# Mixing products interleaved one by one with attention head pairs

## The chip, the cores and the metric

The kernel runs on one core of a Trainium2 chip. Of its engines five matter here: TensorE (PE in the profile, with PEld for its weight loads), VectorE (DVE), ScalarE (ACT), GpSimd (POOL), and the DMA queues, of which SyncE's (SP) carries the transposing transfers and the output. The engines run side by side, each through its own list of instructions in order, and wait for each other through semaphores. The metric is the device time of one execution in microseconds. Before the change it is 171.31 us, the median of three runs (171.11 to 171.92).

## The reference: what is computed

Two layers follow each other, on a batch of 4, with 8 heads, 768 positions and a head width of 64 (model width 512).

The first is an attention in which each position sees its last 96 positions and the first 8, with a bias that falls linearly with the distance:

```python
scores = scale * np.matmul(q, k.transpose(0, 1, 3, 2))
keep = is_global | is_local            # first 8 positions, or 0 <= i - j < 96
scores = np.where(keep, scores + bias, -1000000000.0)
a = np.exp(scores - np.max(scores, axis=-1, keepdims=True))
a = a / (np.sum(a, axis=-1, keepdims=True) + 1e-09)
x = np.matmul(a, v)                    # heads side by side: (4, 768, 512)
```

The second mixes positions and then channels:

```python
theta = x @ w_theta
zr, zi = x * np.cos(theta), x * np.sin(theta)
y = np.einsum('ts,bsd->btd', w_tok_r, zr) + np.einsum('ts,bsd->btd', w_tok_i, zi)
u = x + y
out = u + np.maximum(u @ w_ch, 0.0)
```

## The kernel before, in words

Positions are cut into six tiles of 128, channels into four blocks of 128. All matrix work is in bfloat16 and adds up in PSUM, the memory that only TensorE's matmuls write and that VectorE and ScalarE read.

**Attention of a head pair.** For two heads at a time, `att_transpose` turns q and k (64 wide, so two heads share the 128 rows); ScalarE copies the result out of PSUM (line 232, two copies) and GpSimd makes a variant of the keys with the 8 global positions in front (lines 257 and 258). Since each query tile sees only its own and the previous key tile, the scores are eleven 128 x 128 blocks per head, in three groups (`GROUPS`): group 0 for query tiles 0 and 1, group 1 for tiles 2 and 3, group 2 for tiles 4 and 5. `att_scores` (line 297) computes a group for both heads in one PSUM tile, ScalarE takes the exponential (line 306), and VectorE multiplies by a precomputed mask (lines 317 and 319). `att_values` multiplies the probabilities by the values (line 346, 22 matmuls of 65 columns; the 65th column gives the sum), and VectorE divides (lines 353 and 354).

**Mixing.** `mix_theta` and `mix_z` make the cosine and sine products. `mix_tok` builds an output tile of 128 positions out of twelve matmuls of 512 columns (six source tiles times real and imaginary part; line 430). I call such a matmul a product. When a tile has its twelve, VectorE adds x (line 435), which makes u, and the SP queue transposes u by DMA. `mix_ch` takes four more such products with `w_ch` (line 472), VectorE adds and clips (line 475), and SP writes the result out.

**The order of the work.** `K` keeps the program order on every engine, so the order of the calls in the source is the order of execution. The mixing of batch b is laid beside the attention of batch b + 1, for b = 0, 1, 2. I call these three pieces stretches 1, 2 and 3; each goes through four head pairs. `tok_units` lists the mixing as units, each of four products of a tile (or all four of a `mix_ch`), and `attend_beside` hands them out with `m(n)`:

- ahead of the first pair: three units (twelve products) in stretches 2 and 3, none in stretch 1;
- in each pair: first score group, then two units (one in the first pair), then score groups 1 and 2, the transposes of the next pair, two units (all but one of those left in the last pair), the values;
- behind the last pair: the last unit.

In stretches 2 and 3 the list begins with eight products of tile 0 and eight of tile 1, then the last four of tile 0, the last four of tile 1, then tiles 2 to 5 in turn, with `mix_ch(0)` behind tile 3 and `mix_ch(1)` behind tile 4. In stretch 1 tiles 0 and 1 have ten of their twelve products from earlier, so the list begins with two products of each.

**PSUM buffers.** Mixing tiles and `mix_ch` tiles take turns in two buffers (`ps_mm`, from `ps_acc`), so a tile's first product waits until VectorE has read the tile before the last. Scores, values and `mix_theta` share two wider ones (`ps_w`, from `ps_wide`). Behind each stretch come `mix_ch(2)`, the transposes of the last quarter of x (`turn_x`, line 378), `mix_ch(3)`, and then `mix_theta` for the next batch.

The functions that the change touches:

Of the kernel before, what the change touches and what calls it, by code (L numbers as in the profile page):

```python
# [16 lines left out]
def kernel(  # L17
# [14 lines left out]
    B, H, S, D = q.shape  # L32
    T = 128
    NT = S // T
# [24 lines left out]
    def ps_acc():  # L59
        return psum.tile([T, DM], FP, name="ps_mm", tag="ps_mm", bufs=2)  # L60
# [264 lines left out]
    def att_values(b, h0, apart=False):  # L325

        if h0 == 0:
            x_sb[b] = mbuf.tile([T, NC, NT, T], BF, name="x_sb", bufs=2)
            xTs[b] = mbuf.tile([T, NC, S], BF, name="xT", bufs=2)
        xp = x_sb[b][:, h0 // 2, :, :]  # L330
        vs, vp = v_sb[b % 2], v_pv[b % 2]
        po = None if apart else ps_wide()
        for hh in range(2):
            h = h0 + hh
            ph = ps_acc() if apart else po[:, hh, :]
            for it in range(NT):
                dst = ph[:, it * (D + 1):(it + 1) * (D + 1)]
                mms = []
                if it >= 1:
                    g_, i_ = where[(it, 1)]  # L340
                    rhs = vs[:, h, 0, :] if it == 1 else vp[:, h, it - 2, :]
                    mms.append((probs[b, h0, g_][:, hh, i_ * T:(i_ + 1) * T], rhs))
                g_, i_ = where[(it, 0)]
                mms.append((probs[b, h0, g_][:, hh, i_ * T:(i_ + 1) * T], vs[:, h, it, :]))
                for i_, (lhsT, rhs) in enumerate(mms):
                    K(nc.tensor.matmul(dst, lhsT=lhsT, rhs=rhs,  # L346
                                       start=(i_ == 0), stop=(i_ == len(mms) - 1)))
            if apart:
                values[b, h] = ph
        if not apart:  # L350
            pv = po[:, :, 0:NT * (D + 1)].rearrange("a h (t d) -> a h t d", d=D + 1)
            rec = abuf.tile([T, 2, NT, 1], FP, name="rec")
            K(nc.vector.reciprocal(rec, pv[:, :, :, D:D + 1]))
# [14 lines left out]
    def turn_x(b, dc, by_dma, eng=nc.vector.tensor_copy):  # L368

        xT = xTs[b][:, dc, :]  # L370
        if by_dma:
            K(nc.sync.dma_start(out=xT.rearrange("a (c t) -> a c t", t=T),
                                in_=x_sb[b][:, dc, :, :].rearrange("a t d -> a (t d)"),
                                transpose=True))
            return
        pt = ps_tr(S)
        for st in range(NT):
            K(nc.tensor.transpose(pt[:, st * T:(st + 1) * T], x_sb[b][:, dc, st, :], ident))  # L378
# [81 lines left out]
        for s2 in range(n):  # L460
            uTs[b, tt + s2] = (uT, n, s2)

    def mix_ch(b, tt, cuts=(DM,)):
        uT, n, s2 = uTs[b, tt]
        out_t = out[b].rearrange("(t p) d -> p t d", p=T)[:, tt, :]
        for c0, c1 in zip((0,) + cuts, cuts):
            N = c1 - c0
            cols = slice(c0, c1)
            pc = ps_acc()
            for dc in range(NC):  # L470
                c = (n * dc + s2) * T
                K(nc.tensor.matmul(pc[:, 0:N], lhsT=uT[:, c:c + T], rhs=w_ch_bf[:, dc, cols],  # L472
                                   start=(dc == 0), stop=(dc == NC - 1)))
            o_sb = mbuf.tile([T, N], FP, name="o_sb", bufs=4)
            K(nc.vector.scalar_tensor_tensor(o_sb, in0=pc[:, 0:N], scalar=0.0,  # L475
                                             in1=us[b][:, tt, cols], op0=ALU.max, op1=ALU.add))
            K(nc.sync.dma_start(out=out_t[:, cols], in_=o_sb))


    def tok_units(b, lead):  # L480


        L = []

        def piece(tt, s0):
            L.append(lambda: mix_tok(b, tt, PAIRS[s0:s0 + 4]))

        for tt in (0, 1):
            for s0 in (0, 4) if lead else ():
                piece(tt, s0)  # L490
        for tt in range(NT):
            if tt > 1:
                for s0 in (0, 4, 8):
                    piece(tt, s0)
            elif lead:
                piece(tt, 8)
            else:
                L.append(lambda tt=tt: mix_tok(b, tt, [(4, 1), (5, 1)]))
            if tt in (3, 4):
                L.append(lambda tt=tt: mix_ch(b, tt - 3))  # L500
        return L

    def attend_beside(b, main, lead, load):


        def m(n=1):
# [24 lines left out]


    for h in range(H):
# [71 lines left out]
    for b in range(B):  # L605
        if b == B - 1:
            main = tok_units(b, True)
            main.insert(-1, lambda: mix_uT(b, 4, 1, "act"))
# [58 lines left out]
```

## Time and profile before

| | |
|---|---|
| median of three runs | 171.31 us (171.11 to 171.92) |
| the profiled execution | 171.33 us, of which 169.5 us are the profile's span |
| TensorE matmuls busy | 158.7 us, 94% of the span |
| VectorE busy | 114.7 us, 68% |
| ScalarE busy | 103.0 us, 61% |
| GpSimd busy | 63.2 us, 37% |
| mean granted clock of TensorE | 1.00 |
| products of line 430, 288 in all | 67.0 us |

A line of the chain or of the timeline gives the start in microseconds from the start of the span, a duration, the engine, what it writes or reads with the line of the kernel, and how many instructions are put together. A matmul's duration there is longer than its share of the engine, because matmuls overlap; the distance between starts tells what one costs. Some matmul records are missing from a trace, so a row can say seven where the program has eight. Where the start of an engine's piece is given in square brackets with an arrow, the engine was idle for that time and the name tells what ended it.

The stretches run, from the first scores of their first pair to the end of the values of their last pair, from 39.47 to 62.05 us, from 75.20 to 98.38 us and from 111.53 to 134.38 us.

### The profile page before, as it was taken

What the parts mean: (1) busy time and instruction counts of PE and PEld (TensorE: products, weight loads), DVE (VectorE), ACT (ScalarE), POOL (GpSimd) and SP (SyncE); (2) the same over time, 40 slices, a digit from 0 to 9 for tenths busy, and PEclk for the clock granted to TensorE, in tenths of its full rate; (3) what the DMA queues carried; (4) which work ended last, traced back from release to release, by engine and by line L of the source; (5) the groups of instructions that cost most, each with busy time, mean ns of one, the idle gap of its engine ahead of it and who ended that gap; (6) DMA issues with size and microseconds to landing.
All of it is one profiled execution on the core that took longest, in us unless ns stands there. A gap on an engine that the chain in (4) does not pass through costs nothing.

```text
span 169.5 us, 4624 instructions
## 1 busy us (share of the span) xinstructions
PE 158.7 (94%) x1965; PEld 86.2 (51%) x1988; DVE 114.7 (68%) x210; ACT 103.0 (61%) x120; POOL 63.2 (37%) x99
## 2 busy tenths in 40 slices
PE   7779999999899999999999999999999999999992
PEld 2346665555465654446555554445655544444440
DVE  7768875965858875767587694849568756534362
ACT  4989887957686562798658615996765618300010
POOL 8996797004484650032972900054245000000000
PEclk9999999999999999999999999999999999999999
DMA  4999999999999999910599999711953342121325
GB/s 148 194 180 190 209 211 208 198 180 182 158 140 196 141 173 215 257 70 4 92 145 170 155 187 197 210 62 37 73 110 95 99 148 86 68 60 34 113 102 186
DMA packets 57060, 24.08 MB, mean 142 GB/s; under 512 B 43088, under 2 KB 54096, under 8 KB 57040
## 3 DMA queue, kind: packets, MB, share of 16 engines
q0 software_dynamic: 35328, 12.45, 65.5%
q1 hardware_dynamic: 21440, 10.95, 31.2%
q10 hardware_dynamic: 272, 0.39, 0.7%
q8 instruction: 15, 0.25, 0.6%
q14 instruction: 5, 0.04, 0.1%
HBM read 25.69 MB, written 6.29 MB: 189 GB/s over the span
## 4 chain that ended last, share of the span: by engine, by line
PE 80%; DVE 6%; DMA 4%; issue 3%; POOL 3%; ACT 3%; DVEq 0%; ACTq 0%; POOLq 0%
PE ps_mm L430 35%; PE ps_mm L472 12%; PE ps_w L395 11%; PE ps_w L297 7%; PE ps_w L346 5%; DMA v_sb<-in_v_dram 4%; PE ps_tr L226 3%; PE ps_mm L346 2%; ACT e L306 2%; PE ps_tr L114 2%; DVE zri L411 1%; DVE w_tokT L117 1%; PE ps_tr L378 1%; DVE p L319 1%; ACT qk L249 1%
## 5 line engine op out<-in xcount | busy, mean ns | idle before, releaser
L430 PE MATMUL ps_mm<-zri,w_tokT 128*128 128x512 bf16 x276 | 67.0, 380 | 1.3 <-issue 0.8
L306 ACT ACTIVATE e<-ps_w 128x1024 bf16<-128x1024 f32 (+1 forms) x40 | 37.1, 958 | 17.8 <-PE ps_w L297 17.8
L430 PEld LDWEIGHTS <-w_tokT 128*128 128x128 bf16 x288 | 26.2, 98 | 30.3 <-issue 2.3
L257 POOL COPY qk<-qk 128x512 bf16<-128x512 bf16 x15 | 9.5, 636 | 65.2 <-ACT qk L232 53.0
L319 DVE TENSOR_TENSOR p<-e,wmask 128x1024 bf16<-128x1024 bf16 x28 | 19.9, 712 | 11.8 <-ACT e L306 11.8
L403 ACT ACTIVATE cs<-ps_w,halfpi 128x1024 bf16<-128x1024 f32 x12 | 13.4, 1116 | 18.6 <-PE ps_w L395 18.6
L435 DVE TENSOR_TENSOR u<-x_sb,ps_mm 128x512 bf16<-128x512 bf16 x24 | 16.2, 683 | 12.2 <-PE ps_mm L430 12.2
L395 PE MATMUL ps_w<-w_theta_bf,xT 128*128 128x512 bf16 x91 | 22.6, 379 | 0.6 <-ACT cs L404 0.3
L411 DVE TENSOR_TENSOR zri<-cs,x_sb 128x1024 bf16<-128x1024 bf16 x24 | 16.1, 688 | 9.1 <-ACT cs L403 7.7
L472 PE MATMUL ps_mm<-w_ch_bf,uTd 128*128 128x512 bf16 x82 | 21.5, 379 | 0.6 <-issue 0.5
L297 PE MATMUL ps_w<-qk 64*128 64x128 bf16 (+1 forms) x320 | 16.1, 223 | 2.3 <-DVE qk L249 0.8
L475 DVE SCALAR_TENSOR_TENSOR o_sb<-ps_mm,u 128x512 f32<-128x512 f32 (+2 forms) x25 | 16.5, 664 | 1.1 <-PE ps_mm L472 0.9
L232 ACT COPY qk<-ps_tr 128x768 bf16<-128x768 bf16 x21 | 16.0, 815 | 2.0 <-issue 2.0
L297 PEld LDWEIGHTS <-qk 64*128 64x128 bf16 x320 | 10.0, 94 | 12.1 <-issue 7.8
L346 PEld LDWEIGHTS <-p 128*128 128x128 bf16 x352 | 13.2, 97 | 4.6 <-DVE p L319 0.8
L395 PEld LDWEIGHTS <-xT 128*128 128x128 bf16 x96 | 9.0, 98 | 10.8 <-issue 0.5
L80 POOL DMA_DIRECT2D v_sb<-in_v_dram x10 | 13.0, 1299 | 0.0
L472 PEld LDWEIGHTS <-uTd 128*128 128x128 bf16 x88 | 8.2, 98 | 9.0 <-issue 0.2
L404 ACT ACTIVATE cs<-ps_w 128x1024 bf16<-128x1024 f32 x12 | 12.2, 1020 | 0.0
L92 POOL COPY v_pv<-v_sb 8x520 bf16<-8x520 bf16 x15 | 11.5, 767 | 0.9
L354 DVE TENSOR_TENSOR x_sb<-ps_w,rec 128x768 bf16<-128x768 f32 x12 | 11.5, 958 | 0.4
L346 PE MATMUL ps_w<-v_sb,p 128*128 128x65 bf16 x168 | 11.3, 193 | 0.0
(84 smaller groups left out, 180.2 us busy)
## 6 DMA issues: line engine op xcount, KB each, us to landing
out_dram<-o_sb SPq DMA_DIRECT2D x23, 256.0 KB, 2.3
q_sb<-in_q_dram POOLq DMA_DIRECT2D x6, 384.0 KB, 6.2
k_sb<-in_k_dram POOLq DMA_DIRECT2D x6, 384.0 KB, 9.0
v_sb<-in_v_dram POOLq DMA_DIRECT2D x6, 384.0 KB, 13.5
w_nat<-in_moe_w_tok_r_dram POOLq DMA_DIRECT2D x1, 1152.0 KB, 12.3
w_nat<-in_moe_w_tok_i_dram POOLq DMA_DIRECT2D x1, 1152.0 KB, 13.4
v_sb<-in_v_dram POOLq DMA_DIRECT2D x4, 192.0 KB, 6.7
q_sb<-in_q_dram POOLq DMA_DIRECT2D x3, 192.0 KB, 5.9
```

Source lines behind the costliest of these rows:

```text
L232: K(op(out=qk[:, 0:2 * S].rearrange("a (i r p t) -> a i r p t", i=2, r=2, t=NT)[:, :, r, :, :], in_=halves[r].rearrange("a (i t p) -> a i ...
L297: K(nc.tensor.matmul(ps[:, hh, i_ * T:(i_ + w) * T], lhsT=keys[R, :], rhs=qT[R, it * T:(it + w) * T], start=not bias, stop=not bias or i_ ...
L306: K(nc.scalar.activation(e[:, :, 0:n * T], ps[:, :, 0:n * T], AF.Exp, scale=scale))
L319: K(nc.vector.tensor_mul(p.rearrange("a h (r x) -> a h r x", r=2), e.rearrange("a h (r x) -> a h r x", r=2), wmask[:, hs, None, T:3 * T].t ...
L346: K(nc.tensor.matmul(dst, lhsT=lhsT, rhs=rhs, start=(i_ == 0), stop=(i_ == len(mms) - 1)))
L395: K(nc.tensor.matmul(pth[:, s2, :], lhsT=xTs[b][:, dc, c:c + T], rhs=w_theta_bf[:, dc, :], start=(dc == 0), stop=(dc == NC - 1)))
L403: K(nc.scalar.activation(cs[:, :, 0, :], pth, AF.Sin, bias=halfpi))
L411: K(nc.vector.tensor_mul(zris[b][:, st:st + 2, wi, :].rearrange("a s (c d) -> a s c d", d=T), cs[:, :, wi, :].rearrange("a s (c d) -> a s ...
L430: K(nc.tensor.matmul(acc, lhsT=w_tokT[wi][:, st, tt * T:(tt + 1) * T], rhs=zris[b][:, st, wi, :], start=(done[b, tt] == 0), stop=(done[b, ...
L435: K(nc.vector.tensor_add(us[b][:, tt, :].rearrange("a (c d) -> a c d", d=T), x_sb[b][:, :, tt, :], acc.rearrange("a (c d) -> a c d", d=T)))
L472: K(nc.tensor.matmul(pc[:, 0:N], lhsT=uT[:, c:c + T], rhs=w_ch_bf[:, dc, cols], start=(dc == 0), stop=(dc == NC - 1)))
L475: K(nc.vector.scalar_tensor_tensor(o_sb, in0=pc[:, 0:N], scalar=0.0, in1=us[b][:, tt, cols], op0=ALU.max, op1=ALU.add))
```

## The change: what it does

Three things are changed, all of them in the order of instructions.

The mixing units become single products. `tok_units` lists each product by itself, and `mix_ch` can do one of its four products at a time (it keeps its PSUM tile in `pcs` between calls, and adds and writes behind the fourth).

`attend_beside` takes, for each head pair, how many products stand between the first and the second score group (`n1`) and how many ahead of the values (`n2`), and puts one more product behind the values. Stretches 2 and 3 have 12 products ahead, then (6, 9), (6, 9), (6, 9) and (6, 13), each with one more; stretch 1 has (2, 10), (6, 9), (6, 9) and (6, 8), each with one more.

`att_values`, in the stretches, first does query tiles 0 to 3 of both heads, which need score groups 0 and 1, and then tiles 4 and 5 of both heads, which need group 2. Before the stretches (`apart`) its order stays.

```diff
@@ att_values
-        for hh in range(2):
+        phs = [ps_acc() if apart else po[:, hh, :] for hh in range(2)]
+        parts = (range(NT),) if apart else (range(NT - 2), range(NT - 2, NT))
+        for hh, its in [(hh, its) for its in parts for hh in range(2)]:
             h = h0 + hh
-            ph = ps_acc() if apart else po[:, hh, :]
-            for it in range(NT):
+            ph = phs[hh]
+            for it in its:
@@ mix_ch
-    def mix_ch(b, tt, cuts=(DM,)):
+    def mix_ch(b, tt, cuts=(DM,), d0=0, d1=NC):
...
-            pc = ps_acc()
-            for dc in range(NC):
+            if d0 == 0:
+                pcs[b, tt] = ps_acc()
+            pc = pcs[b, tt]
+            for dc in range(d0, d1):
...
+            if d1 < NC:
+                continue
@@ tok_units
-        def piece(tt, s0):
-            L.append(lambda: mix_tok(b, tt, PAIRS[s0:s0 + 4]))
-        for tt in (0, 1):
-            for s0 in (0, 4) if lead else ():
-                piece(tt, s0)
+        def tile_(tt, P):
+            L.extend((lambda p=p: mix_tok(b, tt, [p])) for p in P)
+        for tt in (0, 1) if lead else ():
+            tile_(tt, PAIRS[0:8])
         for tt in range(NT):
             if tt > 1:
-                for s0 in (0, 4, 8):
-                    piece(tt, s0)
-            elif lead:
-                piece(tt, 8)
+                tile_(tt, PAIRS)
             else:
-                L.append(lambda tt=tt: mix_tok(b, tt, [(4, 1), (5, 1)]))
+                tile_(tt, PAIRS[8:12] if lead else [(4, 1), (5, 1)])
             if tt in (3, 4):
-                L.append(lambda tt=tt: mix_ch(b, tt - 3))
+                L.extend((lambda tt=tt, d=d: mix_ch(b, tt - 3, d0=d, d1=d + 1))
+                         for d in range(NC))
@@ attend_beside
-        for h0 in range(0, H, 2):
+        for h0, (n1, n2) in zip(range(0, H, 2), beside):
             att_scores(b, h0, 0)
-            m(2 if h0 else 1)
+            m(n1)
             att_scores(b, h0, 1)
             att_scores(b, h0, 2)
...
-                m(2)
-            else:
-                if load:
-                    turn_x(b, NC - 2, False)
-                m(len(main) - 1)
+            elif load:
+                turn_x(b, NC - 2, False)
+            m(n2)
             att_values(b, h0)
+            m(1)
...
-        m()
+        assert not main
@@ the loop over batches
-        attend_beside(b + 1, tok_units(b, b > 0), 3 if b else 0, b + 2 < B)
+        if b:
+            attend_beside(b + 1, tok_units(b, True), 12, ((6, 9), (6, 9), (6, 9), (6, 13)), b + 2 < B)
+        else:
+            attend_beside(1, tok_units(0, False), 0, ((2, 10), (6, 9), (6, 9), (6, 8)), True)
```

In the last batch, which has no attention beside it, the products keep their order.

More of the change, by code (lines that the diff above doesn't have):

```diff
@@ L347, in att_values @@
                                        start=(i_ == 0), stop=(i_ == len(mms) - 1)))
-            if apart:
-                values[b, h] = ph
-        if not apart:
+        if apart:
+            values[b, h0], values[b, h0 + 1] = phs
+        else:
             pv = po[:, :, 0:NT * (D + 1)].rearrange("a h (t d) -> a h t d", d=D + 1)
@@ L461, in mix_uT @@
             uTs[b, tt + s2] = (uT, n, s2)
-    def mix_ch(b, tt, cuts=(DM,)):
+    pcs = {}
+    def mix_ch(b, tt, cuts=(DM,), d0=0, d1=NC):
         uT, n, s2 = uTs[b, tt]
@@ L483, in tok_units, with attend_beside, m @@
         L = []
-        def piece(tt, s0):
-            L.append(lambda: mix_tok(b, tt, PAIRS[s0:s0 + 4]))
-        for tt in (0, 1):
-            for s0 in (0, 4) if lead else ():
-                piece(tt, s0)
+        def tile_(tt, P):
+            L.extend((lambda p=p: mix_tok(b, tt, [p])) for p in P)
+        for tt in (0, 1) if lead else ():
+            tile_(tt, PAIRS[0:8])
         for tt in range(NT):
             if tt > 1:
-                for s0 in (0, 4, 8):
-                    piece(tt, s0)
-            elif lead:
-                piece(tt, 8)
+                tile_(tt, PAIRS)
             else:
-                L.append(lambda tt=tt: mix_tok(b, tt, [(4, 1), (5, 1)]))
+                tile_(tt, PAIRS[8:12] if lead else [(4, 1), (5, 1)])
             if tt in (3, 4):
-                L.append(lambda tt=tt: mix_ch(b, tt - 3))
-        return L
-    def attend_beside(b, main, lead, load):
-        def m(n=1):
+                L.extend((lambda tt=tt, d=d: mix_ch(b, tt - 3, d0=d, d1=d + 1))
+                         for d in range(NC))
+        return L
+    def attend_beside(b, main, lead, beside, load):
+        def m(n):
             for _ in range(n):
@@ L607 @@
             main = tok_units(b, True)
-            main.insert(-1, lambda: mix_uT(b, 4, 1, "act"))
+            main.insert(-4, lambda: mix_uT(b, 4, 1, "act"))
             for unit in main:
@@ L616 @@
             break
-        attend_beside(b + 1, tok_units(b, b > 0), 3 if b else 0, b + 2 < B)
+        if b:
+            attend_beside(b + 1, tok_units(b, True), 12, ((6, 9), (6, 9), (6, 9), (6, 13)), b + 2 < B)
+        else:
+            attend_beside(1, tok_units(0, False), 0, ((2, 10), (6, 9), (6, 9), (6, 8)), True)
         mix_ch(b, 2)
```

## The prediction

> **What bounds the kernel now.** I read the page's busy rows first, then its chain, then the chain piece by piece for stretch 2 (attention of batch 2 beside the mixing of batch 1), then the vector and scalar engines in the same microseconds.
>
> ```profile
> PE 158.7 (94%) x1965; PEld 86.2 (51%) x1988; DVE 114.7 (68%) x210; ACT 103.0 (61%) x120; POOL 63.2 (37%) x99
> PE 80%; DVE 6%; DMA 4%; issue 3%; POOL 3%; ACT 3%; DVEq 0%; ACTq 0%; POOLq 0%
> ```
>
> TensorE is busy for 94% of the 169.5 us span and carries 80% of the chain. What can be won is idle time between its instructions; what can be lost is any wait put in front of one, because its matmuls run in the written order. The chain through the second head pair of stretch 2:
>
> ```profile
> 80.26 0.34 PE ps_w L297 x4
> 80.60 1.83 PE ps_mm L430 x8
> 82.44 0.55 PE ps_w L297 x16
> 82.99 0.51 PE ps_tr L226 x48
> 83.49 0.16 issue
> 83.65 1.67 PE ps_mm L430 x7
> 85.33 0.83 PE ps_w L346 x22
> 86.16 0.03 issue
> 86.19 0.34 PE ps_w L297 x4
> ```
>
> This is one step: first scores, eight products, second and third scores, transposes, eight products (one record is missing, hence x7 and the "issue"), values, next first scores. It takes 86.19 - 80.26 = 5.93 us. The values take 0.83 us here and 0.67 in the stretch's last pair (below): the chain names nothing, but the timeline of matmuls has a hole of 0.18 us at the eighth, where the others follow in 0.03; that is the probabilities of the third score group arriving. And the scalar engine shows what holds the step together:
>
> ```profile
> 82.81 1.94 ACT L306 ACTIVATE e<-ps_w 128x1024 bf16<-128x1024 f32 x2 [1.36 <-PE ps_w L297]
> 84.63 1.51 ACT L232 COPY qk<-ps_tr 128x768 bf16<-128x768 bf16 x2
> 86.57 0.81 ACT L306 ACTIVATE e<-ps_w 128x768 bf16<-128x768 f32 x1 [0.43 <-PE ps_w L297]
> ```
>
> The second scores start at 82.37 in the timeline; two exponentials and two copies end at 86.14, and the next first scores, which read those copies, start at 86.19. In all nine places where one pair follows another the distance is 3.82 us (76.44 to 80.26, 88.30 to 92.12, 40.64 to 44.46, and so on), whatever stands between. So a step is (first scores to second scores) + 3.82, and TensorE has a little slack.
>
> ```profile
> 77.93 0.69 DVE L319 TENSOR_TENSOR p<-e,wmask 128x1024 bf16<-128x1024 bf16 x1 [0.61 <-ACT e L306]
> 78.85 0.69 DVE L319 TENSOR_TENSOR p<-e,wmask 128x1024 bf16<-128x1024 bf16 x1 [0.22 <-ACT e L306]
> 79.46 1.28 DVE L435 TENSOR_TENSOR u<-x_sb,ps_mm 128x512 bf16<-128x512 bf16 x2
> 80.65 0.23 DVE L353 RECIPROCAL rec<-ps_w 128x12 f32<-128x12 f32 x1
> ```
>
> This is the vector engine in the first pair of stretch 2, and the line that decides my forecast. The two u additions, which empty the accumulators of mixing tiles 0 and 1, stand behind both multiplications by the mask, although tile 0's products were finished well before. The first is over at 79.46 + 0.68 = 80.14, that is 3.70 us after the second scores (76.44).
>
> ```profile
> 97.88 0.67 PE ps_w L346 x22
> 98.55 0.86 PE ps_mm L430 x4
> 99.41 0.86 PE ps_mm L472 x4
> 100.28 0.34 PE ps_tr L378 x6
> ```
>
> The end of the stretch: values, four products, four of mix_ch(2), six transposes; mix_ch(3) begins at 100.46, 2.08 us after the values (which end at 98.38 by starts).
>
> **The change part by part.** All counts of matmuls, exponentials, copies and DMAs stay; only places move. A product costs 0.216 us (the eight from 83.43 to 85.16). Times below are start to start.
>
> 1. *Six products, not eight, ahead of the second scores.* First to second scores is 82.37 - 80.26 = 2.11; with six 2.11 - 0.43 = 1.68.
>
> 2. *Nine products ahead of the values, one behind, values in two parts.* Second scores to values was 85.16 - 82.37 = 2.79 with eight, so 3.01 with nine. Fourteen of 22 value matmuls need no third group and take 0.44; the late ones begin 3.45 after the second scores, and the probabilities are there after 3.16 (85.53 - 82.37). The stall of 0.15 goes; values cost 0.67. The product behind them costs 0.216, and the switch from products to scores 0.10 (72.51 to 75.20 is 2.69 for twelve products, 12 x 0.216 = 2.59). Sum 3.01 + 0.67 + 0.32 = 3.99. That passes the scalar chain's 3.82, so TensorE becomes the bound: a step is 1.68 + 3.99 = 5.67, a gain of 0.26. Bounds of the one thing not seen before, a lone product between values and scores: 0.32 as taken, or 0.216 plus the whole 0.23 from the last value to scores (85.96 to 86.19), 0.13 more, in nine places 1.2 at most; part of that 0.23 is the wait for the copies, so I stay at the lower end.
>  [...]
>
> 3. *What the earlier second scores meet.* They need the pair's normalised bank: reciprocal and multiplication end 1.44 after the values (98.38 to 99.82), the scores come 0.32 + 1.68 = 2.00 after: covered by 0.5. Their keys come from GpSimd within 0.95 of the copies' end (86.14 to 87.08), which leaves about 0.9. Nothing here, about +0.1 per step if the cover were gone.
>
> 4. *First pair of stretches 2 and 3: 6 + 9 + 1 products in place of 4 + 8.* Twelve products were led in, as before. Tiles 0 and 1 need 24, so they are full after the sixth of the nine, and the seventh opens tile 2. There are two accumulator banks; tile 2 takes tile 0's, so its first product waits for the u addition of tile 0. In the built program that product carries a wait on the vector engine and stands ahead of the values. Before, tile 2 opened only at 80.53, behind the values, 0.39 after the addition's end. Now: second scores at 0; 0.55 + 0.51 + 6 x 0.216 = 2.36 to the sixth product; the addition ends at 3.70, TensorE goes on at 3.76 (0.06 as from 85.47 to 85.53). A new stall of 1.40. Behind it are queued three products (0.65), the values (0.67), the lone product and switch (0.32), then all the rest; the masks' waits vanish in it. The pair takes 1.68 + 3.76 + 0.65 + 0.67 + 0.32 = 7.08 against 5.06 (75.20 to 80.26): +2.02, of which four more products are 0.86.
>
> 5. *The stretches.* Stretch 2, first scores to the values' end, was 98.38 - 75.20 = 23.18. First pair +2.02, two middle pairs 2 x -0.26, last pair (eight + twelve products become six + thirteen, one moves behind) -0.21: +1.29. Stretch 3 (111.53 to 134.38) has the same first pair and steps and a last pair of -0.20: +1.30. Stretch 1 has tiles 0 and 1 all but full from before, so only 2 and 2 products are left, tile 0's addition runs ahead of the masks (41.16), and there is no such wait. Its first pair held the values up for 0.42 (43.80) and was 4.99; with ten products in front it is 1.17 + 4.21 = 5.38, +0.39 for five more products; two middle pairs -0.52; the last pair was 5.73 (56.32 to 62.05) and becomes 1.68, then 3.16 to the probabilities and 0.26 for eight late values, 5.10: -0.63. Sum -0.76.
>
> 6. *The stretch's end.* One product instead of four follows the values, so three more are over beforehand (counted in 5). TensorE would reach mix_ch(3) after 5 x 0.216 + 0.35 = 1.43. It does not: its bank is freed by the last u addition, which runs behind the normalisation and ends 2.03 after the values (99.73 + 0.68 - 98.38). Mix_ch(3) stays at 2.08, and the three moved products gain nothing there: a new idle time of 0.65 each, already in the sum.
>
> 7. *Queues.* GpSimd's list is the same. SP issues one transposing DMA of x after one of u in stretch 1; each takes some 1.2 us, and x is read many microseconds later. The out-DMAs follow their tiles. Nothing; at worst a few tenths if x's transpose were late for theta.
>
> Sum: -0.76 + 1.29 + 1.30 = +1.83. The profiled execution took 171.33 (span 169.5 and 1.8 around it), the median is 171.31; 171.33 + 1.83 = 173.2.
>
> **Rivals.** *Faster: the wait for tile 0's bank is covered.* If the addition were done by the time the sixth product ends, 2 x 1.40 falls away and the time is 170.4. For it: no product of line 430 waits for the additions today. Against it: the addition's place behind the second mask is fixed in the program, and the mask waits for an exponential that ends 2.4 after the second scores. It decides once the stall is under 0.45 per stretch, where the -0.76 pays for both.
>  *The gains do not come.* If the lone product costs its upper end (+1.2), or something keeps the six middle steps at 5.93 (+1.6), the time is 174.4 to 174.8. For it: every step today is 5.93 to the hundredth. Against it: that distance is 2.11 + 3.82, and the 2.11 falls by two products.
>  *The clock.* If TensorE slowed in the 1.4 us holes, the next eight products would run at the rate of the warm-up ones at the start (line 137: 4.4 us for ten, 0.44 each): 8 x 0.22 = 1.8 twice, 176.8. Against it: granted clock 1.00 everywhere, also over the 0.42 hole. [...]
>  *It cancels.* A stall of half the size leaves 173.2 - 1.4 = 171.8.
>
> **How the numbers follow.** Forecast 0.75, faster rival 0.09, gains missing 0.08, clock 0.03, cancels 0.05. The likeliest time is 173.2, its own range 172.6 to 174.0. Eight in ten: from 171.8, where it cancels and short of the faster rival, to 174.5, with the gains in part missing. A measurement tells 0.5% from no change, 170.45 to 172.17: faster 0.09, same 0.06, slower 0.85.
>
> **What would show it.** In the profile after: in the first pair of stretches 2 and 3 a wait of TensorE at line 433 for the u addition of about 1.4 us, the pair at 7.1; middle pairs at 5.67 with no hole in the values; mix_ch(3) still 2.08 behind the values; stretch 1 about 0.76 shorter. Wrong would be: no such wait (then 170.4), middle pairs still at 5.93, or a granted clock below 1.00 behind the holes.

## The result

| | |
|---|---|
| before, median of six runs | 171.42 us (171.11 to 171.92) |
| after, median of six runs | 174.09 us (173.41 to 174.55) |
| ratio, with its 95% interval | 1.0149 (1.0122 to 1.0176) |
| profiled execution of after | 174.55 us, of which 172.8 us are the profile's span |

Here and below a median holds every execution, while a ratio leaves out any that was over 1.5% longer than the fastest of its kernel.

The changed kernel is slower by 1.5%. The forecast was 173.2 us; the time lies inside the range given (171.8 to 174.5) and 0.1 above the likeliest case's own range (172.6 to 174.0). Most of the prediction's steps can be read off the new trace to a few hundredths; one event of about 1.0 us in stretch 2 was not in it.

### The profile after

First the page of the kernel after: busy times, the chain's shares by engine, and the row of the products.

```profile
PE 160.4 (93%) x1988; PEld 84.0 (49%) x1988; DVE 115.6 (67%) x210; ACT 103.0 (60%) x120; POOL 62.4 (36%) x99
PE 78%; DVE 8%; DMA 4%; issue 3%; POOL 3%; ACT 2%; DVEq 0%; ACTq 0%; POOLq 0%
L433 PE MATMUL ps_mm<-zri,w_tokT 128*128 128x512 bf16 x288 | 70.1, 380 | 2.6 <-DVE u L438 2.5
```

Line 433 was line 430. Its row ended with "1.3 <-issue 0.8" before; now 2.5 us of idle time in front of products are put down to the u addition, line 438. VectorE's share of the chain went from 6% to 8%. The page does not say where, so here is the chain through the first pair of stretch 2 (start, length, what it writes, how many):

```profile
75.03 0.27 PE ps_w L297 x4
75.30 1.40 PE ps_mm L433 x6
76.70 0.55 PE ps_w L297 x16
77.26 0.57 PE ps_tr L226 x48
...
78.00 1.03 ACT e L306
...
79.05 0.69 DVE p L319
79.74 0.61 DVE u L438
...
80.39 0.81 PE ps_mm L433 x3
81.20 0.67 PE ps_w L349 x22
```

From the transposes on, the chain leaves TensorE: exponential, mask, u addition, and only then the last three of the nine products. VectorE's timeline in the same place shows the order that forces it:

```profile
78.13 0.69 DVE L319 TENSOR_TENSOR p<-e,wmask 128x1024 bf16<-128x1024 bf16 x1 [1.18 <-ACT e L306]
79.05 0.69 DVE L319 TENSOR_TENSOR p<-e,wmask 128x1024 bf16<-128x1024 bf16 x1 [0.22 <-ACT e L306]
79.66 1.28 DVE L438 TENSOR_TENSOR u<-x_sb,ps_mm 128x512 bf16<-128x512 bf16 x2
81.90 0.23 DVE L356 RECIPROCAL rec<-ps_w 128x12 f32<-128x12 f32 x1 [0.97 <-PE ps_w L349]
```

The additions stand behind both masks as they did before, but now TensorE stands still for the first of them. The sixth and seventh product are 1.60 us apart instead of 0.216, a wait of 1.39; stretch 3 has the same, 1.39.

A middle pair, the second of stretch 2, and ScalarE in the same time:

```profile
82.08 0.27 PE ps_w L297 x4
82.35 1.40 PE ps_mm L433 x6
83.75 0.55 PE ps_w L297 x16
84.31 0.51 PE ps_tr L226 x48
84.81 2.05 PE ps_mm L433 x9
86.86 0.67 PE ps_w L349 x22
87.53 0.22 PE ps_mm L433
87.75 0.21 PE ps_w L297
```

```profile
84.12 1.94 ACT L306 ACTIVATE e<-ps_w 128x1024 bf16<-128x1024 f32 x2 [0.92 <-PE ps_w L297]
85.95 1.51 ACT L232 COPY qk<-ps_tr 128x768 bf16<-128x768 bf16 x2
```

The step is 87.75 - 82.08 = 5.67 us instead of 5.93, the values take 0.67 without a hole, and the chain stays on TensorE throughout: the copies end at 87.46 and the next scores start at 87.68 in the timeline, 0.2 later.

The end of stretch 2:

```profile
99.89 0.69 PE ps_w L349 x22
...
100.60 0.24 DVE rec L356
...
100.87 0.04 DVE x_sb L357
100.91 0.84 issue
101.74 0.69 DVE u L438
...
102.48 0.38 PE ps_mm L480
```

The chain that was one of TensorE's work (values, products, mix_ch(2), transposes) now goes through the normalisation and the last u addition; mix_ch(3) begins at 102.48, still 2.08 after the values. And last, TensorE's timeline in the third pair of stretch 2, which the prediction did not have:

```profile
90.24 0.20 PE L226 MATMUL ps_tr<-ident,k_sb 64*64 64x64 bf16 x4
91.27 0.22 PE L226 MATMUL ps_tr<-ident,q_sb 64*64 64x64 bf16 x4 [0.82 <-issue]
```

In the middle of a run of 48 transposes that otherwise follow each other within 0.51 us, TensorE stops, by starts for 1.02 us, and no semaphore is named.

By starts, the profiled executions' spans differ like this:

| piece | before, us | after, us | difference | forecast |
|---|---|---|---|---|
| up to stretch 1 | 39.47 | 39.90 | +0.43 | 0 |
| stretch 1 | 22.59 | 21.80 | -0.79 | -0.76 |
| between 1 and 2 | 13.14 | 13.28 | +0.13 | 0 |
| stretch 2 | 23.19 | 25.43 | +2.25 | +1.29 |
| between 2 and 3 | 13.14 | 13.14 | 0.00 | 0 |
| stretch 3 | 22.85 | 24.09 | +1.24 | +1.30 |
| behind stretch 3 | 35.15 | 35.15 | -0.01 | 0 |
| span | 169.53 | 172.78 | +3.25 | +1.83 |

The 0.43 ahead of stretch 1 can't be put down to the change: in the fourteen profiled executions of this study stretch 1 begins anywhere from 39.25 to 40.05, the same kernel included (39.89 and 39.25 in two runs of one kernel). The three stretches alone differ by 2.70, which is what the medians differ by (2.67).

### The profile page after: what moved, and what is told of

Read it like the earlier page. It is cut to its first block, busy times and chain, and to the rows that moved or that the text cites. A ratio compares the mean times of both kernels' runs of the same rounds, so it can differ in the third digit from the quotient of the medians.

```text
span 172.8 us, 4655 instructions
## 1 busy us (share of the span) xinstructions
PE 160.4 (93%) x1988; PEld 84.0 (49%) x1988; DVE 115.6 (67%) x210; ACT 103.0 (60%) x120; POOL 62.4 (36%) x99
## 4 chain that ended last, share of the span: by engine, by line
PE 78%; DVE 8%; DMA 4%; issue 3%; POOL 3%; ACT 2%; DVEq 0%; ACTq 0%; POOLq 0%
PE ps_mm L433 35%; PE ps_w L398 11%; PE ps_mm L480 11%; PE ps_w L297 7%; PE ps_w L349 5%; DMA v_sb<-in_v_dram 4%; PE ps_tr L226 4%; DVE w_tokT L117 2%; DVE u L438 2%; PE ps_mm L349 2%; PE ps_tr L114 1%; DVE zri L414 1%; ACT e L306 1%; PE ps_tr L381 1%; ACT qk L249 1%
## 5 line engine op out<-in xcount | busy, mean ns | idle before, releaser
L433 PE MATMUL ps_mm<-zri,w_tokT 128*128 128x512 bf16 x288 | 70.1, 380 | 2.6 <-DVE u L438 2.5
L480 PE MATMUL ps_mm<-w_ch_bf,uTd 128*128 128x512 bf16 x88 | 23.5, 379 | 0.2
L297 PEld LDWEIGHTS <-qk 64*128 64x128 bf16 x320 | 9.2, 94 | 14.0 <-issue 7.1
L349 PEld LDWEIGHTS <-p 128*128 128x128 bf16 x352 | 12.6, 97 | 3.2
L92 POOL COPY v_pv<-v_sb 8x520 bf16<-8x520 bf16 x15 | 10.7, 711 | 0.9
L317 DVE TENSOR_TENSOR p<-e,wmask 128x768 bf16<-128x768 bf16 x12 | 7.1, 596 | 5.0 <-ACT e L306 4.0
```

Source lines behind the costliest of these rows:

```text
L297: K(nc.tensor.matmul(ps[:, hh, i_ * T:(i_ + w) * T], lhsT=keys[R, :], rhs=qT[R, it * T:(it + w) * T], start=not bias, stop=not bias or i_ ...
L349: K(nc.tensor.matmul(dst, lhsT=lhsT, rhs=rhs, start=(i_ == 0), stop=(i_ == len(mms) - 1)))
L433: K(nc.tensor.matmul(acc, lhsT=w_tokT[wi][:, st, tt * T:(tt + 1) * T], rhs=zris[b][:, st, wi, :], start=(done[b, tt] == 0), stop=(done[b, ...
```

## The experiments

The kernels below start from the kernel after. To vary the number of products behind a pair's values, `attend_beside` takes it as a third number; all products are always done. Times are compared with runs of the kernel before on the same chip.

### The kernel after once more

No edit.

> The changed kernel once more, with another profile. The theory (in the first pair of stretches 2 and 3 tile 2's first product waits for the u addition of tile 0, which stands behind both masks) expects the same two waits of 1.39 us. Open is the hole of 1.0 us that the first profile has inside the transposes of the third pair of stretch 2, with nothing that it waits for: if it belongs to the order of instructions it comes again at the same place, and the median stays at 174.1; if it is chance, it is gone here or stands elsewhere, and an execution without it takes 173.1 to 173.6.

Measured: 174.48 us, ratio 1.0153 (1.011 to 1.0195). Both waits are there (1.39 each), and the hole in the third pair's transposes too, at the same four transposes, 0.93 long by starts. So the hole came in both profiles of this order of work and is no accident of one execution.

### Tile 0 closed first

```diff
-        for tt in (0, 1) if lead else ():
-            tile_(tt, PAIRS[0:8])
+        if lead:
+            tile_(0, PAIRS[0:8])
+            tile_(1, PAIRS[0:4])
+            tile_(0, PAIRS[8:12])
+            tile_(1, PAIRS[4:12])
...
-            else:
-                tile_(tt, PAIRS[8:12] if lead else [(4, 1), (5, 1)])
+            elif not lead:
+                tile_(tt, [(4, 1), (5, 1)])
```

All counts stay; tile 0 gets its last four products before tile 1 its last eight (in the last batch, too, where nothing stands beside the mixing; the time behind stretch 3 is 35.1 us in both).

> All counts as in the changed kernel, but tile 0's last four products are done ahead of tile 1's last eight, so that tile 0 is full ahead of the second scores and its u addition runs ahead of the masks on the vector engine. The product that opens tile 2 keeps its place ahead of the values. The theory expects its wait gone, because the addition now ends some 2 us sooner: 170.4 to 171.3. The rival that opening a tile ahead of the values costs by itself, whatever the addition's place, expects 173.5 to 174.1.

Measured: 170.59 us, ratio 0.9933 (0.9906 to 0.996): faster than before, and 3.7 us less than the kernel after by the two ratios (two waits of 1.39 and the hole are 3.8). VectorE's timeline in the first pair of stretch 2:

```profile
77.03 0.68 DVE L438 TENSOR_TENSOR u<-x_sb,ps_mm 128x512 bf16<-128x512 bf16 x1
78.41 0.69 DVE L319 TENSOR_TENSOR p<-e,wmask 128x1024 bf16<-128x1024 bf16 x1 [0.70 <-ACT e L306]
79.33 0.69 DVE L319 TENSOR_TENSOR p<-e,wmask 128x1024 bf16<-128x1024 bf16 x1 [0.22 <-ACT e L306]
79.94 0.68 DVE L438 TENSOR_TENSOR u<-x_sb,ps_mm 128x512 bf16<-128x512 bf16 x1
```

Only tile 1's addition is left behind the masks (x1, not x2); tile 0's, at 77.03, runs ahead of them. The first pair takes 5.66 us instead of 7.05, and the hole in the third pair is gone as well. In the list only a few products of tiles 0 and 1 change places, so that the addition that frees tile 2's bank comes earlier, and this turns the slowdown into a gain: the wait is shown to be the cause of 2 x 1.39, and with it comes the hole (tested further below).

### Tile 2 opened later, by the counts alone

```diff
-            attend_beside(b + 1, tok_units(b, True), 12, ((6, 9), (6, 9), (6, 9), (6, 13)), b + 2 < B)
+            attend_beside(b + 1, tok_units(b, True), 12, ((6, 6, 1), (6, 9, 1), (6, 9, 1), (6, 16, 1)), b + 2 < B)
```

> In the first pair of stretches 2 and 3 six products instead of nine stand ahead of the values, so that tile 2 opens behind them; the three go to the last pair (16 ahead of its values). The theory expects both waits gone: 2 x 1.39 less than the changed kernel, 171.3 beside its 174.1, and 170.4 where no hole comes in. The rival, that the loss comes from the cut into single products (a lone product between values and scores, more switches), expects no gain, 173.5 or more, since all of that stays.

Measured: 180.45 us, ratio 1.0485 (1.0421 to 1.0549). The expectation missed by nine to ten microseconds, and the miss is instructive. The waits of TensorE from 74 to 100 us (in total, times, longest):

```profile
PE ps_mm L433 <- DVE u L438: 3.7, 3, 2.1
```

The first pair's wait has shrunk to 0.34, but the three products pushed back shift everything behind. Now the closing products of tiles 3 and 4 fall ahead of the values, so that their u additions stand behind the masks of their pair, and the first products of tiles 4 and 5, which stand in the same place, wait: 1.60 and 2.24 us by starts in stretch 2, 1.60 and 2.11 in stretch 3, 7.6 us together. I had counted where the openings go, not where the closings go. No hole turns up in the transposes here.

### Counts that keep closings ahead of the masks

```diff
-            attend_beside(b + 1, tok_units(b, True), 12, ((6, 9), (6, 9), (6, 9), (6, 13)), b + 2 < B)
+            attend_beside(b + 1, tok_units(b, True), 12, ((6, 6, 1), (6, 9, 1), (7, 8, 1), (7, 15, 1)), b + 2 < B)
```

> The list's order as in the kernel after, only counts of stretches 2 and 3 differ: (6, 6), (6, 9), (7, 8), (7, 15), one more behind each, so that tile 2's first product stands behind the first pair's values, and the closing products of tiles 3 and 4 stand in the piece ahead of the second scores, their u additions ahead of the masks. Theory (a first product waits when, and only when, the u addition that frees its bank stands behind the masks of the same pair): no wait over 0.1 us at any tile's first product, and the time is that of the run with tile 0 first, 170.4 to 171.2 (the first pair's values with six products ahead stall up to 0.4 in two stretches). Rival (opening a tile close behind the closing of the tile before the last costs a wait in any order, and the run with tile 0 first gained by its shorter way to the first addition): waits of 1 us and more stay, 173 or more.

Measured: 172.04 us, ratio 1.0000 (0.9971 to 1.003). Tiles 3 and 4, closed ahead of the second scores, cause no wait any more: from a ratio of 1.0485 to 1.0000 by moving one product in each of two pairs. The time is 1.2 above the run with tile 0 first by the two ratios, more than expected, nearly all of it in the first pairs: their values take 1.39 instead of 0.67, with a hole of 0.36 for the third group's probabilities (only six products cover them) and one of 0.34 ahead of the product behind them. That is tile 2's first, which still waits there for tile 0's addition; I had expected no wait over 0.1. Tile 0 is closed behind the second scores here as in the kernel after, and the rest of the wait is what the values leave of it.

### The change in stretch 1 alone

```diff
-            attend_beside(b + 1, tok_units(b, True), 12, ((6, 9), (6, 9), (6, 9), (6, 13)), b + 2 < B)
+            attend_beside(b + 1, tok_units(b, True), 12, ((4, 8, 0), (8, 8, 0), (8, 8, 0), (8, 12, 4)), b + 2 < B)
```

Stretches 2 and 3 have the counts of before, in single products; the values' new order stays everywhere.

> The change in stretch 1 alone: stretches 2 and 3 have the counts of before (12, then 4 and 8, 8 and 8, 8 and 8, 8 and 12, four behind the last values). The values' new order is in all stretches. The theory expects stretch 1 shorter by 0.8 us and the others as before, 170.6 beside 171.4. The rival of the single products expects stretch 1 no shorter, 171.4 or more.

Measured: 171.3 us beside 171.92, ratio 0.9965 (0.9932 to 0.9997), 0.6 us less (0.05 to 1.2). Where no bank is waited for, the change gains what the prediction gave for that stretch (0.76); the interval is too wide to tell the two figures apart. In the profile stretch 1 takes 21.80 us instead of 22.59, and stretches 2 and 3 take 23.19 and 22.85 as before.

### The next batch loaded later

```diff
-                if load and h0 == 0:
+                if load and h0 == 2:
```

> The kernel after with one change: the next batch's q, k and v are loaded one head pair later (second pair of the stretch, not the first). Theory (the hole of about 1.0 us in the third pair's transposes of stretch 2 is TensorE waiting for its own next piece of program, whose 16 KB packet runs at 88.8 us in the same DMA engines as those loads; the 1.39 us wait in the first pair moves TensorE's demand behind the loads' start): no hole there, stretch 2 as long as stretch 3, 24.1 to 24.5 us in place of 25.43; the two waits of 1.39 us for tile 0's bank stay; time 173.1 to 173.5 where the kernel after has 174.1. Rival (the hole has another cause, in the transposes or in the order of products): it stays at its place, stretch 2 at 25.4 and the time at 174.1. Third possibility: the loads only move onto another fetch, and a hole of about 1 us turns up elsewhere.

Measured: 173.5 us, ratio 1.0069 (1.0033 to 1.0104), against 1.0149 for the kernel after: 1.4 us less by the two ratios. TensorE's instructions are the same ones in the same order. The two waits for tile 0's bank stay (gaps of 1.60 us), the hole is gone, and stretch 2 takes 24.43 us (25.43 after; the prediction's sum for it was 24.47). The same transposes in its chain:

```profile
89.83 0.51 PE ps_tr L226 x48
...
90.50 0.38 PE ps_mm L480
```

What moved with the loads is a 16 KB packet of kind "instruction". In the kernel after it runs at 88.77 us, for 1.11, among the loads' packets (first fence: its queues from 88 to 90 us, packets, MB, share of the 16 engines); with the loads later it runs at 85.31, and there are no loads then (second fence, 85 to 87 us):

```profile
q0 software_dynamic: 443, 0.34, 109.7%
q1 hardware_dynamic: 304, 0.07, 19.1%
q8 instruction: 1, 0.02, 3.5%
```

```profile
q1 hardware_dynamic: 189, 0.04, 10.3%
q8 instruction: 1, 0.02, 4.7%
```

In the run with tile 0 first it ran at 84.30, in the kernel before at 83.98, just ahead of the loads. TensorE's weight loads all have a record (x1988 in the pages of before and after, where the matmuls' rows have x1965 and x1988), so its progress can be counted by them. In the twelve profiles without the hole the packet ran when 1143 to 1149 of them had started; in the two of the kernel after when 1183 had, and the hole stands behind the 1245th in both. In the kernel after the 1146th starts at 85.19 us, 1.2 us after the loads' first packet; in the twelve others that packet came 0.5 us ahead of it at most. This fits the following account, which is my inference from these counts: a piece of program is ordered when TensorE has got to a certain point; in the kernel after, the wait of 1.39 us brings that point behind the start of the loads, the piece comes some 3.5 us later than with the loads out of the way, and TensorE runs dry. That the loads' place makes the hole is shown by this run. That the link is a piece of TensorE's program is inferred: there are 15 such packets in the run, and beside TensorE's 1988 matmuls and as many weight loads no engine has more than 210 instructions of work in its row. The packet is over at 89.88 and TensorE goes on at 91.27; what passes in the 1.4 us between, the trace does not show.

The third possibility in the expectation came true in another form: later loads are in the way of something else. Ahead of a mix_ch behind stretch 2 TensorE loses 0.85 us, and the chain there is one transposing transfer of u that took 9.11. (This profiled execution, 174.3 us, is the slowest of the ten; what the faster ones have in this place has no trace, so the 1.4 us can't be divided between hole and transfer to the tenth.)

```profile
95.61 9.11 DMA uTd<-u
...
104.77 1.04 PE ps_mm L480 x4
```

### No product between values and scores

```diff
-            attend_beside(b + 1, tok_units(b, True), 12, ((6, 9), (6, 9), (6, 9), (6, 13)), b + 2 < B)
+            attend_beside(b + 1, tok_units(b, True), 12, ((6, 10, 0), (6, 10, 0), (6, 10, 0), (6, 13, 1)), b + 2 < B)
-            attend_beside(1, tok_units(0, False), 0, ((2, 10), (6, 9), (6, 9), (6, 8)), True)
+            attend_beside(1, tok_units(0, False), 0, ((2, 11, 0), (6, 10, 0), (6, 10, 0), (6, 8, 1)), True)
```

The list has tile 0 first.

> The same mixing list (tile 0 first), but no product between the values and the next first scores: ten products ahead of the values, none behind, in the nine places where a pair follows another; the last pairs keep theirs. All products are kept. Theory of the prediction (changing from products to scores costs 0.10 us, changing from values to scores 0.10 to 0.23): the step of a middle pair is 1.68 + 0.55 + 0.51 + 2.16 + 0.67 + (0.10 to 0.23) = 5.67 to 5.80, the whole 170.6 to 171.8, against 170.6 with the lone product. Rival (the lone product itself saves or costs more than a switch, as it covers the copies that the next scores read): the scalar chain of 3.82 binds again with 3.99 available, so nothing of it, step 5.67 to 5.70; or the step is under 5.6 and the lone product was a loss.

Measured: 170.89 us, ratio 0.9936 (0.9899 to 0.9974), beside 0.9933 with the lone product. Middle pairs take 5.67 with and without it. The last value matmul is followed by the next scores after 0.125 us, where values follow each other in 0.03, so this switch costs 0.10, what it costs behind a product (0.312 - 0.216). The product that the change puts between a pair's values and the next scores is worth nothing in either direction.

### The values' new order alone, and the old order with nine products

First edit, with the counts and the list's order of the kernel before:

```diff
-            attend_beside(b + 1, tok_units(b, True), 12, ((6, 9), (6, 9), (6, 9), (6, 13)), b + 2 < B)
+            attend_beside(b + 1, tok_units(b, True), 12, ((4, 8, 0), (8, 8, 0), (8, 8, 0), (8, 12, 4)), b + 2 < B)
-            attend_beside(1, tok_units(0, False), 0, ((2, 10), (6, 9), (6, 9), (6, 8)), True)
+            attend_beside(1, tok_units(0, False), 0, ((2, 6, 0), (8, 8, 0), (8, 8, 0), (8, 8, 4)), True)
```

> The counts and the list's order of the kernel before (8 products ahead of the second scores, 8 ahead of the values, none behind), with one part of the change alone: the values in two parts, query tiles 0 to 3 of both heads first. Theory (prediction, part 2: a step is the way from first to second scores plus 3.82 of exponentials and copies): the hole of 0.15 in the values goes, and the same time turns up ahead of the next first scores; middle pairs stay at 5.93, the time within 0.2 of before (ratio 0.998 to 1.001). Rival (the hole in the values is what a step loses): middle pairs at 5.78, six of them, 0.9 less, ratio 0.995.

Measured: 171.5 us, ratio 0.9998 (0.9968 to 1.0029). Middle pairs stay at 5.93; the values run through, and the next scores wait instead. Only the last pair of stretch 1 gains, 5.52 instead of 5.73. The chain through the second pair of stretch 2 says for what:

```profile
83.92 1.02 ACT e L306
84.94 1.41 ACT qk L232 x2
86.34 0.04 issue
86.39 0.27 PE ps_w L297
```

Second edit, on the run with tile 0 first:

```diff
-        parts = (range(NT),) if apart else (range(NT - 2), range(NT - 2, NT))
-        for hh, its in [(hh, its) for its in parts for hh in range(2)]:
+        parts = (range(NT),)
+        for hh, its in [(hh, its) for hh in range(2) for its in parts]:
```

> The run with tile 0 first (which was faster than before, 170.6), with the values in their old order, head by head. Theory (nine products cover the third score group by themselves: values begin 3.01 behind the second scores, their ninth matmul, which reads the third group, 3.23, and the probabilities are there after 3.16): middle pairs stay at 5.67 and only the last pair of stretch 1, with eight products, loses 0.2; 170.6 to 170.9, ratio 0.993 to 0.995. Rival (the new order is what closes the hole): each of nine pairs loses 0.15 or more, 172.0, ratio 1.000.

Measured: 170.42 us, ratio 0.9946 (0.9918 to 0.9974). Middle pairs 5.67, and the one place that loses is the last pair of stretch 1, whose values take 1.00 instead of 0.79. In the middle pairs the order of the values is worth nothing, neither while eight products leave the step to the copies nor when nine cover the probabilities; in all it is worth the 0.2 us of that last pair.

### Four products behind the last values

```diff
-            attend_beside(b + 1, tok_units(b, True), 12, ((6, 9), (6, 9), (6, 9), (6, 13)), b + 2 < B)
+            attend_beside(b + 1, tok_units(b, True), 12, ((6, 9, 1), (6, 9, 1), (6, 9, 1), (6, 10, 4)), b + 2 < B)
-            attend_beside(1, tok_units(0, False), 0, ((2, 10), (6, 9), (6, 9), (6, 8)), True)
+            attend_beside(1, tok_units(0, False), 0, ((2, 7, 1), (6, 9, 1), (6, 9, 1), (6, 8, 4)), True)
```

The list has tile 0 first. It was run twice.

> The mixing list with tile 0 closed before tile 1 goes on (no wait for its bank, as in the run that was faster than before) and, in each stretch, four products behind the last pair's values instead of one. Theory (prediction, part 6: the last mix_ch of a stretch begins 2.08 us behind the values, whatever stands in between, because its bank is freed only then): the three products moved behind the values fill the idle 0.65 us of each stretch's end, mix_ch(3) stays at 2.08, and the stretches lose up to 3 x 0.65 = 1.9 us, less about 0.15 in the first pair of stretch 1, which has three products fewer to cover the probabilities: 168.8 to 169.1, a ratio of about 0.984 to before. Rival (the end of the u addition moves with the values' end and the products between delay the normalisation's bank or the transposes): mix_ch(3) moves to 2.7 behind the values and the time stays at 170.6, ratio 0.993.

> The run with four products behind the last values again, beside the plain one on the same chip: ratio 0.984 to 0.988 to before, as its profile's span (167.9, where before has 169.5) says; 0.994, the upper end of its first interval, would say that the profiled execution was a lucky one.

Measured: 169.98 us, ratio 0.9873 (0.9806 to 0.9939), and 169.48 us, ratio 0.9895 (0.9812 to 0.9977). In the second profile the end of stretch 2 is TensorE's work again, with nothing else in its chain:

```profile
95.69 0.67 PE ps_w L349 x22
96.36 0.86 PE ps_mm L433 x4
97.23 0.86 PE ps_mm L480 x4
98.09 0.34 PE ps_tr L381 x6
98.43 0.37 PE ps_mm L480
```

Mix_ch(3) begins 2.07, 2.22 and 2.08 after the values, not 2.7: the idle 0.65 of each stretch's end takes the three products in. In the first run's profile the stretches are 0.39, 0.65 and 0.62 us shorter than with tile 0 first (stretch 1's first pair, with seven products, has a hole of 0.15 in its values). The ratios say 1.0 to 1.3% less than before, a little short of the 1.2 to 1.6% forecast; that it beats the run with tile 0 first is seen in the traces, while the intervals of the two overlap.

### Only the earlier second scores

Old order of the values, no lone product, four products behind the last values, tile 0 first:

```diff
-            attend_beside(b + 1, tok_units(b, True), 12, ((6, 9), (6, 9), (6, 9), (6, 13)), b + 2 < B)
+            attend_beside(b + 1, tok_units(b, True), 12, ((6, 10, 0), (6, 10, 0), (6, 10, 0), (6, 10, 4)), b + 2 < B)
-            attend_beside(1, tok_units(0, False), 0, ((2, 10), (6, 9), (6, 9), (6, 8)), True)
+            attend_beside(1, tok_units(0, False), 0, ((2, 8, 0), (6, 10, 0), (6, 10, 0), (6, 8, 4)), True)
```

> Only two things of all that was changed are kept: six products, not eight, between first and second scores, and counts and list order that close a tile ahead of the masks. The values have their old order, nothing stands between the values and the next first scores, and four products stand behind a stretch's last values. Theory (neither the lone product nor the values' order is worth anything): a span of 167.9 to 168.3 like the run with four products behind the last values, 0.2 more for the values of the first and last pair of stretch 1, ratio to before 0.985 to 0.989. Rival (either of the two matters once the other is gone): middle pairs at 5.8 and more, 171 and more, ratio 0.995.

Measured: 169.85 us, ratio 0.9891 (0.9848 to 0.9933); middle pairs 5.67. Its ten runs spread from 168.84 to 171.34. The profiled one took 171.03 (span 169.2, not the 167.9 to 168.3 expected) and has 0.61 and 1.48 us of idle time ahead of mix_ch behind stretch 2, both ended by a transposed u:

```profile
93.48 9.84 DMA uTd<-u
...
103.36 0.82 PE ps_mm L480 x3
```

Without them the span would be 167.1, an estimate that takes both waits off in full. The values also wait in the last pair of stretch 3 (0.90 instead of 0.69), which the expectation did not have. So of everything that was changed, six products instead of eight ahead of the second scores do the work, once nothing waits for a bank; and what held this execution up next is the transposing transfer beside the loads. That such waits explain the whole spread was not shown, as only one execution has a trace.

## Why the prediction was right, and what it missed

**Parts 1 and 2, the steps.** Forecast 5.67, measured 5.67 in five of the six middle pairs; the sixth is the one with the hole (6.67). The terms are right too: first to second scores 1.67 (1.68), values 0.67, lone product and switch 0.31 (0.32). The choice between the ends for the lone product, 0.32 or 0.13 more, was decided by the run without it: a switch behind values costs 0.10, so the rest of the 0.23 seen before was the wait for the copies, as the prediction took it. The switch comes once per pair in either place, 0.10 behind a product and 0.10 behind values, so the product in between neither removes one nor adds one, and the 1.2 that the rival without gains charged for it is not there. What the prediction did not say is how the gain divides: all of it comes from the two products taken from ahead of the second scores, none from the lone product or the values' order.

**Part 3, cover.** Nothing showed; middle pairs have no idle time ahead of the earlier second scores.

**Part 4, the wait for tile 0's bank.** Forecast 1.40 and 7.08 for the pair; measured 1.39 twice, and 7.05 twice. The run with tile 0 first and the two runs with other counts show the rule behind it: a tile's opening product waits if the closing of the tile that held its bank stands behind the second scores of the same pair, because VectorE then adds behind the masks.

**Part 5, the sums.** Stretch 1 was forecast at -0.76 and is -0.79, stretch 3 at +1.30 and is +1.24. Stretch 2 was forecast at +1.29 and is +2.25. The failed step is the equality of stretches 2 and 3 in its sum: it counted no stall beyond the masks' wait. The missing 0.96 is the hole in the third pair's transposes (1.02 by starts), by the account above, which is inferred, TensorE out of program beside the next batch's loads, which stretch 3 does not have. Add it, and 173.2 becomes 174.2, where 174.09 was measured. That the range reached far enough up for this was luck: its upper end was set for gains that fail to come, and they came.

**Part 6, the stretch's end.** Mix_ch(3) was forecast to stay at 2.08 and is at 2.08, 2.08 and 2.07. The idle 0.65 was real, and putting three products there took up nearly all of it.

**Part 7, queues.** "Nothing" was right of the transposing transfers that it names, and wrong of what it left out: the packets of kind "instruction", which the profile counts on the same 16 DMA engines as the loads (0.6% of their time, and 65.5% for the software queue, in the page of the kernel before). The 1.2 us that it gives for a transposing transfer is SP's time for issuing one; those of u took 2.4 to 8.5 us from issue to landing in the kernel before. The instruction queue was in the page of the kernel before (15 packets, 0.25 MB) and I passed over it.

**The rivals.** The faster case needed the addition ahead of the masks; it did not happen by itself, and the run with tile 0 first, where it was made to, gives a ratio of 0.9933, or 170.2 from 171.31, against that rival's 170.4. The case without gains gave 174.4 to 174.8, near the measured time, but by a mechanism that the trace denies: the middle pairs did gain 0.26. The clock stayed at 1.00 and the products behind the 1.39 us waits follow at 0.216. That eight products would run at 0.44 behind such a hole was an estimate from the ten of line 137, and no run shows it. The longest wait for a bank in these runs, 2.24 us, came in an execution with a mean granted clock of 0.998; no longer one was there.

## What to carry to other kernels

Before an accumulator is opened at a new place, look up in the list of the engine that empties it where the emptying stands; in an in-order list it is late by all that stands ahead of it (the addition of tile 0 started at 79.66 us behind the masks, in the kernel after, and at 77.03 ahead of them, in the run with tile 0 first), and shifting a few products can move the wait to another tile (180 us) or remove it (170.6). When several things change together, find by single runs which of them pays: here moving two products from ahead of the second scores to behind them did everything, and the rest nothing, or it cost time. And count the DMA engines' other customers, the packets of kind "instruction" and the transposes, when a wait moves work relative to a bulk load (here a wait of 1.39 us came with a hole of 1.02).

## What the runs showed of the hardware

Packets of 16 KB and kind "instruction", 15 in a run, run among the data's packets; that they carry TensorE's program is inferred from their number and places. One that ran between 83.32 and 85.31 us in twelve profiles ran at 88.77 and 89.06 in the two of the kernel after, in the midst of software DMA loads, and TensorE stood for 0.93 to 1.02 us with no semaphore named. The transposing transfers took longer beside loads, too. In the kernel before, the six of u issued between 111 and 140 us, where no loads ran, took 2.4 us from issue to landing in the median, and the three issued between 85 and 100 us, beside the loads, 7.7; those that TensorE waited for above took 9.1 and 9.8. A switch of TensorE to the scores' tile shape cost 0.10 us behind products (0.312 - 0.216) and behind values (0.125 - 0.03) alike. And in the rows of the kernels before and after only TensorE writes PSUM; that no other engine could is not shown by them.
